# Split heads' q and k loaded one head beneath the other on 128 partitions, in a planned attention and two-layer MoE kernel

## The chip, the cores and the metric

The kernel runs on one core of a Trainium2 chip. The metric is the device time of one execution in microseconds; 1057.7 us is the median of three runs of the kernel before.

## What is computed

Causal attention with a decay from cumulative logs, then two gated feed-forward layers. Cut to what matters:

```python
B, H, S, D = 4, 8, 576, 64            # q, k, v: (B, H, S, D); f: (B, H, S)
scores = matmul(q, k.T) / sqrt(D)
cum = cumsum(log(clip(f, 1e-4, 1)), -1)
scores = where(causal, -1e9, scores + cum[..., :, None] - cum[..., None, :])
attn = softmax(scores)                 # the sum has 1e-9 added
x = concat_heads(attn @ v)             # (2304, 512)
x = (x @ w_a) * (x @ w_b) @ w_out      # d_ff 1536
xn = x / rms(x) * rms_g
out = silu(xn @ w_gate) * (xn @ w_val) @ w_out2
```

## The kernel before

The 2304 tokens are worked in three chunks of 576, 704 and 1024 columns, and each feed-forward layer runs per chunk as a phase: six phases on TensorE, which multiplies in a fast float format with 32-bit operands split into a high part and a remainder. The attention of batch 0 comes first; the attention of batches 1, 2 and 3 is woven between the matmuls of the phases (the table `ATT`), so that the softmax on VectorE and ScalarE runs beside feed-forward matmuls.

The order of all instructions on all engines is made at build time by the class `Plan`. Every piece of work is handed to `op` with its engine (or several to choose from), an estimated cost in ns, what it reads and writes, and a priority (a time: smaller goes first). `Plan.order` places the pieces one after the other: on each engine the piece that can start first, by estimated ends, latencies between engines, buffers that come free, and a lock between VectorE pieces marked `port=True` and GpSimd. A load is estimated in `run`: it ends at the later of its issue plus 1150 ns and the end of the load before it, plus its `nbytes` over `RATE` = 300 bytes per ns. Every 30,000 ns nine ways of weighing priorities are tried, and the one after which TensorE has done most is kept. All loads and stores are issued by SyncE, in the order of the plan, and a load that waits holds up those behind it.

Attention works by pairs of heads. `plan_attention` calls `heads` for each of the four pairs of a batch, and then `unit`, `packed` and `values`. `heads` makes the tiles of a pair: `b` (one buffer), `qk` (one buffer), `vr` (two). Batch 0 (`sf` true) multiplies 32-bit floats directly, and its q and k go straight into `b`. For the others ("split heads") q and k go into `qk`, and `head` builds from them, for each of the two heads g: `qa` (128 partitions: the high part of q in one half, the remainder of q in the other), `ka` (the high part of k in both halves), and rows 0 to 63 of `b` (high q, and the remainder of k; rows 64 to 67 come from a small load of decay rows). A score is then two matmuls: `qa` by `ka` over 128 rows, that is (high q + remainder of q) by high k, and `b` by `b` over 68 rows, that is high q by the remainder of k, and the decay.

The steps, as the prediction names them: the *loads* (L1889 to L1893, issued at L1873); the *copies*, which make high parts, by ScalarE (L1931) or GpSimd (L1933), whichever the plan expects to end first: first and second copy of q (L1942, L1943), first and second copy of k (L1948, L1949); and the *remainders* on VectorE (L1936): of q (L1944), which reads the first copy of q, and of k (L1950), which reads the second copy of k. Before, `qk` has q of both heads side by side on partitions 0 to 63 and k of both on 64 to 127, so that each load writes 64 partitions with two rows of up to 576 columns each.

Of the kernel before, what the change touches and what calls it, by code (L numbers as in the profile page):

```python
# [30 lines left out]
PE, ACT, DVE, POOL, SP = "PE", "ACT", "DVE", "POOL", "SP"  # L31
# [66 lines left out]
def act(n, psum=False):  # L98
    return (51 if psum else 93) + n / 1.2


def dve(n):
    return 69 + n / 0.96
# [10 lines left out]
def pool1(n):  # L114
    return 135 + n / 0.96
# [61 lines left out]
class Plan:  # L177
# [19 lines left out]
    def op(self, eng, cost, fn, reads=(), writes=(), prio=0.0, after=(), nbytes=0, start=0, port=False, kind=0):  # L197
        n = Node()
        n.port, n.kind = port, kind
        n.eng, n.cost, n.fn, n.prio, n.bytes, n.ready = eng, cost, fn, prio, nbytes, start  # L200
        deps, n.allocs, n.bufs, n.first = set(after), [], set(), set()
        for t in (*reads, *writes):
            b = t[0] if isinstance(t, tuple) and isinstance(t[0], Buf) else t
            if isinstance(b, Buf):
                if b.alloc is None:
                    b.alloc = n
                    n.allocs.append(b)
                    self.rings.setdefault(b.tag, []).append(b)
                elif b.alloc is not n:
                    n.first.add(b.alloc)  # L210
                if b not in n.bufs:
                    n.bufs.add(b)
                    b.users.append(n)
        for t in reads:
            assert t in self.writer, t
            deps.add(self.writer[t])
            self.readers.setdefault(t, []).append(n)
        for t in writes:
            if t in self.writer:
                deps.add(self.writer[t])  # L220
            deps.update(self.readers.get(t, ()))
            self.writer[t] = n
            self.readers[t] = []
        deps.discard(n)
        n.first -= deps
        deps |= n.first
        n.deps, n.outs, n.waiting = deps, [], len(deps)
        for d in deps:
            d.outs.append(n)
        n.given, n.att = (eng, cost, fn, start), False  # L230
        self.nodes.append(n)
        return n
# [153 lines left out]
class Kernel:  # L386
# [1479 lines left out]
    def heads(self, c, h, q0, k1, t, sf):  # L1866

        nc, op = self.nc, self.op
        g0 = c * H + h

        def load(cost, out, src, reads=(), writes=(), dt=0):
            op(
                SP, 600 if cost > 40000 else 320, lambda *_: nc.sync.dma_start(out(), src), reads=reads, writes=writes, prio=t - dt,  # L1873
                nbytes=cost, start=QUIET,
            )

        def of(x, rows, *at):
            return lambda: x.tile[(rows, slice(None), *at)]

        def heads_of(x, *at):  # L1880
            return x[(slice(g0, g0 + 2), *at)].rearrange("h d c -> d h c")

        both = range(2)
        top, dt = (66, F32) if sf else (68, F32R)
        b = self.tile([top, 2, 2, S], "b0", 2, dt, pool=self.early) if c == 0 else self.tile([top, 2, 2, S], "b", 1, dt, pool=self.att)
        qk = None if sf else self.tile([128, 2, S], "qk", 1, pool=self.att)
        vr = self.tile([128, 2, 5, D], "vr", 2, pool=self.att)
        for i, (x, lo) in enumerate(((self.qT, q0), (self.kT, 0))):
            out = of(b, slice(0, 64), i, slice(lo, k1)) if sf else of(qk, slice(64 * i, 64 * i + 64), slice(lo, k1))  # L1889
            load(  # L1890
                768 * (k1 - lo), out, heads_of(x, slice(None), slice(lo, k1)),
                writes=[(b, g, i, 0) if sf else (qk, g, i) for g in both], dt=15000,
            )  # L1893
        if sf:
            for i in both:
                load(
                    9216, lambda i=i: b.tile[64:66, :, i, :], heads_of(self.aux32, slice(i, i + 2), slice(None)),
                    [("aux32", 0), ("aux32", 1)], [(b, g, i, 1) for g in both], 12000,
                )
        else:  # L1900
            load(
                36864, lambda: b.tile[64:68].bitcast(F32).rearrange("p h t c -> p (h t) c"),
                self.aux[g0 : g0 + 2].rearrange("h t r c -> r (h t) c"), [("aux", i) for i in (0, 2, 4)],
                [(b, g, i, 1) for g in both for i in both], 12000,
            )
        nv = min(k1 // 128, 4)
        load(
            65536 * nv, lambda: vr.tile[:, :, 0:nv, :], self.vA[g0 : g0 + 2, :, 0:nv].rearrange("h p b d -> p h b d"),
            writes=[(vr, 0)], dt=11000,
        )  # L1910
        v = [(vr, 0)]
        if k1 > 512:
            load(
                32768, lambda: vr.tile[0:64, :, 4, :], self.vB[g0 : g0 + 2].rearrange("h p d -> p h d"), writes=[(vr, 1)],
                dt=10000,
            )
            v.append((vr, 1))
        return [self.head(g, q0, k1, t + 400 * g, sf, b, qk, vr, v) for g in both]

    def head(self, g, q0, k1, t, sf, b, qk, vr, v):  # L1920

        nc, op = self.nc, self.op
        pair = Slot(lambda: b.tile[:, g, 0]), Slot(lambda: b.tile[:, g, 1])
        own = [(b, g, i, j) for i in range(2) for j in range(2)]
        values = Slot(lambda: vr.tile[:, g]), v
        if sf:
            return [pair], own, values

        def copy(by, out, x):
            if by == ACT:  # L1930
                nc.scalar.activation(out, x, AF.Copy)  # L1931
            else:
                nc.gpsimd.tensor_scalar(out=out, in0=x, scalar1=1.0, scalar2=0.0, op0=ALU.mult, op1=ALU.add)  # L1933

        def rest(out, x, high):
            nc.vector.tensor_tensor(out=out, in0=x, in1=high.bitcast(F32), op=ALU.subtract)  # L1936

        qr, kr = (lambda: qk.tile[0:64, g]), (lambda: qk.tile[64:128, g])
        q, k = (qk, g, 0), (qk, g, 1)
        qa, ka = (self.tile([128, S], x + "a", 2, F32R, pool=self.att) for x in "qk")  # L1940
        n = k1 - q0
        op((ACT, POOL), (act(n), pool1(n)), lambda by, x: copy(by, x[0:64, q0:k1], qr()[:, q0:k1]), reads=[q], writes=[(qa, 0)], prio=t - 9000)  # L1942
        op((ACT, POOL), (act(n), pool1(n)), lambda by, *_: copy(by, b.tile[0:64, g, 0, q0:k1], qr()[:, q0:k1]), reads=[q], writes=[(b, g, 0, 0)], prio=t - 8000)  # L1943
        op(  # L1944
            DVE, dve(n), lambda: rest(qa.tile[64:128, q0:k1], qr()[:, q0:k1], qa.tile[0:64, q0:k1]),
            reads=[q, (qa, 0)], writes=[(qa, 1)], prio=t - 7000, port=True,
        )
        op((ACT, POOL), (act(k1), pool1(k1)), lambda by, x: copy(by, x[0:64, :k1], kr()[:, :k1]), reads=[k], writes=[(ka, 0)], prio=t - 7000)  # L1948
        op((ACT, POOL), (act(k1), pool1(k1)), lambda by, *_: copy(by, ka.tile[64:128, :k1], kr()[:, :k1]), reads=[k], writes=[(ka, 1)], prio=t - 6000)  # L1949
        op(  # L1950
            DVE, dve(k1), lambda: rest(b.tile[0:64, g, 1, :k1], kr()[:, :k1], ka.tile[64:128, :k1]),
            reads=[k, (ka, 1)], writes=[(b, g, 1, 0)], prio=t - 5000, port=True,
        )
        return [(qa, ka), pair], [*own, *((x, i) for x in (qa, ka) for i in range(2))], values

    def unit(self, c, u, heads, t, sf):

        a, e = u
        n, sm, ps = e - a, self.tile([128, 2], "sm", 4, pool=self.att), []
        for g, (pairs, qk, _) in enumerate(heads):  # L1960
            s = self.bank("s", S_BANKS)

            def scores(x, pairs=pairs):
                for j, (q, k) in enumerate(pairs):
                    self.nc.tensor.matmul(  # L1965
                        x[:n, :e], q.tile[:, a:e], k.tile[:, :e], start=j == 0, stop=j == len(pairs) - 1
                    )

            self.op(PE, 4 * e / 2.4 + 3 if sf else 2 * mm(e), scores, reads=qk, writes=[s], prio=t + 400 * g, kind=int(sf))
            p = self.tile([128, S], "P", P_BUFS, pool=self.att)  # L1970
            self.exps(n, e, [self.mask[:, 384 - a : 384 - a + e]], [s], p, sm, g, t + 600 + 400 * g)
            ps.append(p)
        self.norms(n, e, ps, sm, 1, t + 1000)
        return ps
# [192 lines left out]
```

## Time and profile before

| | |
|---|---|
| three runs | 1057.08, 1057.7, 1063.99 us |
| profiled execution, its time | 1057.13 us |
| its span, first to last instruction | 1055.4 us |
| TensorE matmul, busy | 1036.5 us (98%) |
| VectorE, busy | 830.3 us (79%) |
| ScalarE, busy | 605.6 us (57%) |
| GpSimd, busy | 193.2 us (18%) |
| mean granted clock of TensorE | 0.998 |

Busy times are sums over instructions of one engine. The ends of matmuls are modelled, so busy does not mean that TensorE runs at its peak. "PEld" is TensorE's weight load, which overlaps its matmuls. A wait is put down to the work that ended last before the waiting instruction began. The share of the DMA engines is a mean over sixteen; in short stretches it can read a little over 1.

### The profile page before, as it was taken

The page shows a single profiled execution, that of the slowest core. Times are in us where ns is not written, and L with a number is a line of the kernel's source. Part 1 is how long each engine was busy: PE and PEld are TensorE (multiplying, and loading weights), DVE is VectorE, ACT ScalarE, POOL GpSimd, SP SyncE. Part 2 cuts the span into 40 slices and gives each one's busy share as a digit, 9 for nine tenths or more (in the row PEclk, how much of TensorE's full clock was granted, in tenths as well). Part 3 has the DMA queues.
Part 4 walks back from the last instruction along what each step waited for, and adds up shares of the span by engine and source line. Part 5 has one row for each costly group of instructions (what it writes and reads, how often), then busy time and mean ns, then how long its engine had stood idle before and what let it go on. Part 6 is the DMA issues. An engine that isn't in the chain of part 4 may idle for free.

```text
span 1055.4 us, 19131 instructions
## 1 busy us (share of the span) xinstructions
PE 1036.5 (98%) x6716; PEld 931.0 (88%) x6716; DVE 830.3 (79%) x1877; ACT 605.6 (57%) x1324; POOL 193.2 (18%) x203
## 2 busy tenths in 40 slices
PE   9899999999999999999999999999999999999998
PEld 7688998899999998999999999988888887888886
DVE  7877989787597878977899587865568479979974
ACT  8889888755463779955775463532333264444330
POOL 3333333312101243333440010000000001100000
PEclk9999999999999999999999999999999999999999
DMA  7879787879486685787898684786453634546332
GB/s 180 270 246 300 245 284 244 256 238 347 158 295 233 223 281 191 234 281 260 289 319 307 227 282 173 273 278 194 138 180 120 206 115 152 178 130 191 119 118 80
DMA packets 90607, 233.05 MB, mean 221 GB/s; under 512 B 12960, under 2 KB 23408, under 8 KB 90512
## 3 DMA queue, kind: packets, MB, share of 16 engines
q1 hardware_dynamic: 90512, 231.84, 66.6%
q8 instruction: 53, 0.87, 0.3%
q14 instruction: 42, 0.34, 0.1%
HBM read 157.05 MB, written 74.74 MB: 220 GB/s over the span
## 4 chain that ended last, share of the span: by engine, by line
PE 62%; DVE 13%; ACT 9%; DMA 8%; issue 6%; POOL 2%; SPq 0%; DVEq 0%; POOLq 0%; ACTq 0%
PE m L940 15%; PE m L942 14%; PE m L941 14%; PE s L941 2%; PE s L942 2%; PE s L940 2%; ACT P L1562 2%; PE tp L941 2%; PE tp L942 2%; PE tp L940 2%; DMA raw<-wv 2%; DVE w L789 2%; DMA w<-wd 1%; PE tp L2029 1%; PE tp L1603 1%
## 5 line engine op out<-in xcount | busy, mean ns | idle before, releaser
L940 PE MATMUL m<-E,w 128*128 128x512 f32 (+3 forms) x672 | 233.3, 347 | 1.3 <-ACT a L1329 0.7
L942 PE MATMUL m<-E,w 128*128 128x512 f32 (+3 forms) x672 | 228.0, 339 | 0.5 <-POOL w L797 0.5
L941 PE MATMUL m<-E,w 128*128 128x512 f32 (+3 forms) x624 | 213.2, 342 | 0.0
L1329 ACT ACTIVATE a<-m 128x352 f32<-128x352 f32 (+1 forms) x144 | 74.7, 527 | 139.9 <-PE m L942 139.4
L941 PE MATMUL m<-Eb,w 128*128 128x352 f32 (+3 forms) x432 | 140.9, 326 | 0.0
L940 PEld LDWEIGHTS m<-E,w 128*128 128x128 f32 x672 | 127.3, 189 | 15.0 <-issue 1.4
L942 PEld LDWEIGHTS m<-E,w 128*128 128x128 f32 x672 | 126.9, 189 | 11.4 <-POOL w L797 0.9
L797 POOL TENSOR_TENSOR w<-w,w 128x512 fp32r<-128x512 f32 x72 | 97.1, 1354 | 201.7 <-ACT w L1654 161.3
L1338 DVE TENSOR_TENSOR a<-m,a 128x352 f32<-128x352 f32 (+1 forms) x144 | 86.3, 602 | 57.5 <-PE m L942 56.1
L940 PE MATMUL m<-Eb,w 128*128 128x352 f32 (+3 forms) x384 | 127.8, 333 | 1.2 <-ACT a L1329 0.6
L941 PEld LDWEIGHTS m<-E,w 128*128 128x128 f32 x624 | 118.2, 189 | 10.8
L942 PE MATMUL m<-Eb,w 128*128 128x352 f32 (+3 forms) x384 | 126.7, 330 | 0.0
L940 PE MATMUL m<-G,w 128*128 128x352 f32 (+2 forms) x352 | 111.3, 316 | 0.7 <-DVE a L1338 0.4
L941 PE MATMUL m<-G,w 128*128 128x352 f32 (+2 forms) x352 | 108.2, 308 | 0.0
L942 PE MATMUL m<-G,w 128*128 128x352 f32 (+2 forms) x352 | 108.2, 308 | 0.0
L1562 ACT ACTIVATE P<-P,mn 128x512 f32<-128x512 f32 (+4 forms) x128 | 76.3, 597 | 19.2 <-DVE mn L1555 19.0
L941 PEld LDWEIGHTS m<-Eb,w 128*128 128x128 f32 x432 | 81.3, 188 | 4.3
L940 PEld LDWEIGHTS m<-Eb,w 128*128 128x128 f32 x384 | 72.2, 188 | 6.9 <-ACT a L1329 0.8
L942 PEld LDWEIGHTS m<-Eb,w 128*128 128x128 f32 x384 | 72.2, 188 | 4.3
L1465 ACT ACTIVATE G<-a 128x352 fp32r<-128x352 f32 (+3 forms) x100 | 47.1, 473 | 46.1 <-DVE a L1451 17.8
L940 PEld LDWEIGHTS m<-G,w 128*128 128x128 f32 x352 | 66.2, 188 | 2.9 <-issue 1.7
L1555 DVE CUSTOM_DVE_ANT_0 P<-s,mask 128x512 f32<-128x512 f32 (+4 forms) x128 | 61.3, 494 | 9.1 <-PE s L1965 4.2
(264 smaller groups left out, 2262.4 us busy)
## 6 DMA issues: line engine op xcount, KB each, us to landing
w<-wd SPq DMA_DIRECT2D x72, 512.0 KB
wd<-w SPq DMA_DIRECT2D x48, 512.0 KB
ws<-w SPq DMA_DIRECT2D x48, 512.0 KB
w<-ws SPq DMA_DIRECT2D x48, 512.0 KB
w<-wf SPq DMA_DIRECT2D x60, 256.0 KB
wf<-w SPq DMA_DIRECT2D x48, 256.0 KB
raw<-wo SPq DMA_DIRECT2D x24, 512.0 KB
w<-wd SPq DMA_DIRECT2D x44, 256.0 KB
```

Of the source, the lines that this page charges most:

```text
L789: nc.vector.scalar_tensor_tensor(out=x, in0=words(I32, 0), scalar=29, in1=x, op0=ALU.logical_shift_right, op1=ALU.bitwise_or)
L797: nc.gpsimd.tensor_tensor(out=w.tile[:, :, 1, :], in0=i32.tile.bitcast(F32), in1=w.tile[:, :, 0, :].bitcast(F32), op=ALU.subtract)
L940: mm_(o, wh, xh, start=start, stop=False)
L941: mm_(o, wh, xl, start=False, stop=False)
L942: mm_(o, wl, xh, start=False, stop=stop)
L1329: nc.scalar.activation(z[:, :h], bank_.tile[:, :h], AF.Copy)
L1338: nc.vector.tensor_tensor(out=z, in0=bank_.tile[:, :h], in1=z, op=ALU.add)
L1465: nc.scalar.activation(out(0), x(), AF.Copy)
L1555: nc.vector.tensor_tensor_reduce(out=p.tile[:n, i * w : i * w + w], in0=s[i].tile[:n, :w], in1=masks[i][:n], scale=-0.125, scalar=mn.tile[ ...
L1562: nc.scalar.activation(o, o, AF.Exp, bias=mn.tile[:n, len(s) - 1 : len(s)], scale=-1.0, accum_out=sm.tile[:n, g : g + 1])
L1603: nc.tensor.transpose(ps.tile[:w, c : c + n], p.tile[:n, i * 128 : i * 128 + w], self.ident[:n, :n])
L2029: nc.tensor.matmul(x[64 * g : 64 * g + 64, o : o + n], tiles[g][2][0].tile[:k, i, :], y.tile[:k, to : to + n], start=i == 0, stop=i == blo ...
```

## The change

For split heads, q of the pair's two heads is now loaded one head beneath the other: head g lies on partitions 64g to 64g + 63, q in the first half of the tile's columns and k in the second, and each load writes 128 partitions with one row each. The estimate for the plan goes from 768 to 512 bytes per column; the estimated issue (600 ns over 40,000 bytes) stays, as all these loads are above it. In `head`, the high part of a head stands in the half where its raw data lie (`here`) and what is moved across stands in the other (`there`): for the first head that leaves q as it was, for the second head the halves of `qa` change places. The first copy of k goes to `here`, the second to `there`, and the remainder of k reads the first copy instead of the second. Rows 0 to 63 of `b` stay what they were.

```diff
         for i, (x, lo) in enumerate(((self.qT, q0), (self.kT, 0))):
-            out = of(b, slice(0, 64), i, slice(lo, k1)) if sf else of(qk, slice(64 * i, 64 * i + 64), slice(lo, k1))
+            if sf:
+                out, src = of(b, slice(0, 64), i, slice(lo, k1)), heads_of(x, slice(None), slice(lo, k1))
+            else:
+                out = lambda i=i, lo=lo: qk.tile[:, i, lo:k1]
+                src = x[g0 : g0 + 2, :, lo:k1].rearrange("h d c -> (h d) c")
             load(
-                768 * (k1 - lo), out, heads_of(x, slice(None), slice(lo, k1)),
-                writes=[(b, g, i, 0) if sf else (qk, g, i) for g in both], dt=15000,
+                (768 if sf else 512) * (k1 - lo), out, src, writes=[(b, g, i, 0) for g in both] if sf else [(qk, i)], dt=15000,
             )
...
-        qr, kr = (lambda: qk.tile[0:64, g]), (lambda: qk.tile[64:128, g])
-        q, k = (qk, g, 0), (qk, g, 1)
+        here, there = (slice(64 * x, 64 * x + 64) for x in (g, 1 - g))
+        qr, kr = (lambda i=i: qk.tile[here, i] for i in range(2))
+        q, k = (qk, 0), (qk, 1)
...
-            DVE, dve(n), lambda: rest(qa.tile[64:128, q0:k1], qr()[:, q0:k1], qa.tile[0:64, q0:k1]),
+            DVE, dve(n), lambda: rest(qa.tile[there, q0:k1], qr()[:, q0:k1], qa.tile[here, q0:k1]),
             reads=[q, (qa, 0)], writes=[(qa, 1)], prio=t - 7000, port=True,
         )
-        op((ACT, POOL), (act(k1), pool1(k1)), lambda by, x: copy(by, x[0:64, :k1], kr()[:, :k1]), reads=[k], writes=[(ka, 0)], prio=t - 7000)
-        op((ACT, POOL), (act(k1), pool1(k1)), lambda by, *_: copy(by, ka.tile[64:128, :k1], kr()[:, :k1]), reads=[k], writes=[(ka, 1)], prio=t - 6000)
+        op(*by_k, lambda by, x: copy(by, x[here, :k1], kr()[:, :k1]), reads=[k], writes=[(ka, 0)], prio=t - 7000)
+        op(*by_k, lambda by, *_: copy(by, ka.tile[there, :k1], kr()[:, :k1]), reads=[k], writes=[(ka, 1)], prio=t - 6000)
         op(
-            DVE, dve(k1), lambda: rest(b.tile[0:64, g, 1, :k1], kr()[:, :k1], ka.tile[64:128, :k1]),
-            reads=[k, (ka, 1)], writes=[(b, g, 1, 0)], prio=t - 5000, port=True,
+            DVE, dve(k1), lambda: rest(b.tile[0:64, g, 1, :k1], kr()[:, :k1], ka.tile[here, :k1]),
+            reads=[k, (ka, 0)], writes=[(b, g, 1, 0)], prio=t - 5000, port=True,
         )
```

## Rows read from the trace of the kernel before

**Rows 1.** Page, part 1: busy us, share of the span, instructions by engine.

```profile
PE 1036.5 (98%) x6716; PEld 931.0 (88%) x6716; DVE 830.3 (79%) x1877; ACT 605.6 (57%) x1324; POOL 193.2 (18%) x203
```

**Rows 2.** Stretches: length; PE, PEld, DVE, ACT, POOL busy; clock; DMA share, GB/s.

```profile
24.00:79.00 55.00, 52.10 (x432) 40.37 (x431) 45.69 (x128) 44.99 (x106) 19.50 (x19) 0.97 0.83 255
79.00:225.00 146.00, 141.27 (x1188) 132.88 (x1187) 122.41 (x336) 119.41 (x305) 46.32 (x51) 1.00 0.81 261
225.00:350.00 125.00, 124.36 (x840) 121.57 (x839) 94.93 (x236) 66.15 (x149) 17.26 (x22) 1.00 0.72 256
350.00:450.00 100.00, 98.13 (x814) 93.34 (x813) 87.80 (x228) 83.20 (x198) 36.58 (x38) 1.00 0.74 234
450.00:575.00 125.00, 123.88 (x965) 120.79 (x965) 105.85 (x259) 81.10 (x181) 42.83 (x40) 1.00 0.86 294
```

**Rows 3.** Waits of matmuls (PE), weight loads (PEld): us, times, longest.

```profile
PE tp L1603 <- ACT P L1586: 2.1, 3, 1.1
PE s L1965 <- DVE mn L1555: 2.0, 5, 0.7
...
PE m L940 <- DMA w<-wd: 0.6, 2, 0.4
...
PE s L1965 <- DVE b L1936: 0.3, 1, 0.3
...
PEld s L1965 <- DVE b L1936: 0.5, 1, 0.5
```

**Rows 4.** Instructions on tile qk: ns min/median/max, first and last start us, shapes.

```profile
L1936 DVE TENSOR_TENSOR qa<-qk,qa x32: 279/744/1836, 38.0 to 555.7; 64x576 fp32r<-64x576 f32 x16, 64x128 fp32r<-64x128 f32 x8, 64x448 fp32r<-64x448 f32 x8
L1936 DVE TENSOR_TENSOR b<-qk,ka x32: 284/753/1816, 43.4 to 563.7; 64x576 fp32r<-64x576 f32 x24, 64x128 fp32r<-64x128 f32 x8
...
L1873 SPq DMA_DIRECT2D qk<-kT x16: 595/602/610, 24.7 to 516.8; - x16
```

**Rows 5.** DMA issues of tile qk by size.

```profile
qk<-kT SPq DMA_DIRECT2D x12, 288.0 KB
...
qk<-qT SPq DMA_DIRECT2D x8, 288.0 KB
...
qk<-qT SPq DMA_DIRECT2D x4, 224.0 KB
...
qk<-qT SPq DMA_DIRECT2D x4, 64.0 KB
```

**Rows 6.** Stretches as in rows 2, beside and behind a pair's loads.

```profile
362.75:364.25 1.50, 1.50 (x13) 1.43 (x12) 1.44 (x4) 0.39 (x2) 0.00 (x0) 1.00 1.03 415
365.75:367.75 2.00, 1.88 (x12) 1.88 (x13) 2.00 (x8) 0.85 (x2) 0.00 (x0) 1.00 1.01 235
```

**Rows 7.** Waits for the loads of q and k: us, times, longest.

```profile
POOL qa L1933 <- DMA qk<-qT: 2.9, 1, 2.9
...
ACT ka L1931 <- DMA qk<-kT: 0.4, 1, 0.4
```

**Rows 8.** Issues at L1873: the load of v, columns as in rows 4.

```profile
L1873 SPq DMA_DIRECT2D vr<-vA x20: 378/386/1270, 14.2 to 526.2; - x20
```

**Rows 9.** Waits of SyncE's queue: us, times, longest.

```profile
SPq L1873 <- DVE b L1936: 30.6, 10, 8.2
```

**Rows 10.** Wide remainders and copies of k by shape: count, busy us, mean ns, idle before.

```profile
L1936 DVE TENSOR_TENSOR b<-qk,ka 64x576 fp32r<-64x576 f32 x24 | 19.1, 816 | 0.5
L1936 DVE TENSOR_TENSOR qa<-qk,qa 64x576 fp32r<-64x576 f32 x16 | 14.5, 930 | 0.3
...
L1933 POOL TENSOR_SCALAR ka<-qk 64x576 fp32r<-64x576 f32 x23 | 16.5, 715 | 9.7 <-issue 6.1 <-DMA qk<-kT 1.0 <-DMA w<-wd 0.7
...
L1931 ACT ACTIVATE ka<-qk 64x576 fp32r<-64x576 f32 x25 | 16.5, 680 | 0.8 <-DMA qk<-kT 0.4
```

**Rows 11.** Timeline of VectorE and GpSimd near 143 us: start us, us, what.

```profile
143.32 2.68 DVE L1936 TENSOR_TENSOR qa<-qk,qa 64x576 fp32r<-64x576 f32 x2
...
143.72 1.67 POOL L797 TENSOR_TENSOR w<-w,w 128x512 fp32r<-128x512 f32 x1
```

More of the change, by code (lines that the diff above doesn't have):

```diff
@@ L1936, in rest @@
             nc.vector.tensor_tensor(out=out, in0=x, in1=high.bitcast(F32), op=ALU.subtract)
-        qr, kr = (lambda: qk.tile[0:64, g]), (lambda: qk.tile[64:128, g])
-        q, k = (qk, g, 0), (qk, g, 1)
+        here, there = (slice(64 * x, 64 * x + 64) for x in (g, 1 - g))
+        qr, kr = (lambda i=i: qk.tile[here, i] for i in range(2))
+        q, k = (qk, 0), (qk, 1)
         qa, ka = (self.tile([128, S], x + "a", 2, F32R, pool=self.att) for x in "qk")
         n = k1 - q0
-        op((ACT, POOL), (act(n), pool1(n)), lambda by, x: copy(by, x[0:64, q0:k1], qr()[:, q0:k1]), reads=[q], writes=[(qa, 0)], prio=t - 9000)
-        op((ACT, POOL), (act(n), pool1(n)), lambda by, *_: copy(by, b.tile[0:64, g, 0, q0:k1], qr()[:, q0:k1]), reads=[q], writes=[(b, g, 0, 0)], prio=t - 8000)
+        by_q, by_k = ((ACT, POOL), (act(n), pool1(n))), ((ACT, POOL), (act(k1), pool1(k1)))
+        op(*by_q, lambda by, x: copy(by, x[here, q0:k1], qr()[:, q0:k1]), reads=[q], writes=[(qa, 0)], prio=t - 9000)
+        op(*by_q, lambda by, *_: copy(by, b.tile[0:64, g, 0, q0:k1], qr()[:, q0:k1]), reads=[q], writes=[(b, g, 0, 0)], prio=t - 8000)
         op(
-            DVE, dve(n), lambda: rest(qa.tile[64:128, q0:k1], qr()[:, q0:k1], qa.tile[0:64, q0:k1]),
+            DVE, dve(n), lambda: rest(qa.tile[there, q0:k1], qr()[:, q0:k1], qa.tile[here, q0:k1]),
             reads=[q, (qa, 0)], writes=[(qa, 1)], prio=t - 7000, port=True,
         )
-        op((ACT, POOL), (act(k1), pool1(k1)), lambda by, x: copy(by, x[0:64, :k1], kr()[:, :k1]), reads=[k], writes=[(ka, 0)], prio=t - 7000)
-        op((ACT, POOL), (act(k1), pool1(k1)), lambda by, *_: copy(by, ka.tile[64:128, :k1], kr()[:, :k1]), reads=[k], writes=[(ka, 1)], prio=t - 6000)
-        op(
-            DVE, dve(k1), lambda: rest(b.tile[0:64, g, 1, :k1], kr()[:, :k1], ka.tile[64:128, :k1]),
-            reads=[k, (ka, 1)], writes=[(b, g, 1, 0)], prio=t - 5000, port=True,
+        op(*by_k, lambda by, x: copy(by, x[here, :k1], kr()[:, :k1]), reads=[k], writes=[(ka, 0)], prio=t - 7000)
+        op(*by_k, lambda by, *_: copy(by, ka.tile[there, :k1], kr()[:, :k1]), reads=[k], writes=[(ka, 1)], prio=t - 6000)
+        op(
+            DVE, dve(k1), lambda: rest(b.tile[0:64, g, 1, :k1], kr()[:, :k1], ka.tile[here, :k1]),
+            reads=[k, (ka, 0)], writes=[(b, g, 1, 0)], prio=t - 5000, port=True,
         )
```

## The prediction

> **What bounds the kernel now.** I read the busy times first. TensorE is busy 1036.5 of 1055.4 us [rows 1]. The count of matmuls and their shapes depend on no line of this diff, so the change can only touch the 18.9 us in which TensorE stands idle, or add to them. I then cut the span into stretches around the split heads (the first k is loaded at 24.7 us, the last at 516.8, and the last remainder starts at 563.7 us [rows 4]). In [rows 2] the first column after the length is TensorE's busy time, so its idle time is 55.00 - 52.10 = 2.90, 146.00 - 141.27 = 4.73, 125.00 - 124.36 = 0.64, 100.00 - 98.13 = 1.87 and 125.00 - 123.88 = 1.12 us: 11.3 us over the 551 us from 24 to 575. The rest of the idle time lies before 24 us or behind 575 us, where no split head is prepared. Third, the waits of TensorE by releaser: the longest sums are 2.0 and 2.1 us, for the softmax of the attention; the only wait of a matmul for what the diff edits is 0.3 us, once, for the remainder of k, and a weight load, which overlaps matmuls, waits 0.5 us for the same [rows 3]. No row has TensorE waiting for the load of q or k. So the kernel is bound by TensorE's own work, and the edited work has TensorE waiting for fractions of a microsecond.
>
> **The change part by part.**
>
> *The loads.* 32 DMAs: 12 of k and 8 of q with 288 KB, 4 of q with 224 KB, 4 of q and as many of k with 64 KB, that is 20 x 294,912 + 4 x 229,376 + 8 x 65,536 = 7.34 MB [rows 5]. None is added and no byte more is moved; each now spans 128 partitions instead of 64. Does that make them shorter? The stretch 365.75 to 367.75 us follows the issue of a q and a k load, and the DMA engines are full (share 1.01) but move 235 GB/s; 362.75 to 364.25 us, where weights on 128 partitions are under way, is as full and moves 415 GB/s [rows 6]. I take these two as the rates before and after: 294,912 B take 1.25 us, then 0.71 us, 0.54 us less for each wide load, and 7.34 MB take 31.2, then 17.7 us, 13.5 us less of DMA time in all. From below the saving is nothing (if the low rate is due to what else was in flight); I take the measured ratio, since nothing but the span differs in kind. What hides it: the code gives each load a lead of 15,000 ns on its head. Only GpSimd and ScalarE have rows of waiting for them, five rows from 2.9 down to 0.4 us [rows 7], and TensorE has none. What TensorE can get back through the shorter queue is bounded by its waits for any DMA, 0.6 us for a weight tile [rows 3]. I book 0.3 us.
>
> *Their issue on SyncE.* A load of k takes 602 ns to issue [rows 4], one of v, already on 128 partitions, 386 ns [rows 8]. If the new form takes the latter, 32 x 0.216 = 6.9 us of SyncE's queue are saved; if not, nothing. SyncE's queue waits 30.6 us for the remainder of k to release the q and k tile [rows 9]; behind those loads in order stand v, the auxiliary rows and the next weights. All this is slack that TensorE doesn't see (its DMA waits are the same 0.6 us), so it is booked at nothing.
>
> *The copies and remainders.* Per head four copies and two remainders, before as after, with the same shapes; only the partition halves change. Copies from 64-127 to 0-63 exist before; the move from 0-63 to 64-127 by ScalarE or GpSimd is new, and I bound it by the same rows: 680 ns on ScalarE, 715 on GpSimd [rows 10], no reason for another length. Booked at nothing.
>
> *The remainder of k waits for the first copy of k instead of the second.* At best it starts one copy (0.68 to 0.72 us) sooner. TensorE's wait behind it was 0.3 us, so at most 0.3 us comes back. It also loses a protection. The remainder of q already waits for its first copy alone, and takes 930 ns in the wide form, where that of k takes 816 [rows 10]; the longest are 1836 and 1816 ns against medians of 744 and 753 [rows 4]. In the timeline the cause is visible: two remainders of q take 2.68 us from 143.32 to 146.00, beside a GpSimd instruction that runs from 143.72 to 145.39 [rows 11]. Taken at the price of q, the 24 wide remainders of k cost 24 x 0.114 = 2.7 us of VectorE; nothing from below, 24 x (1.816 - 0.816) = 24.0 us from above. VectorE is busy 122.41 of 146 and 87.80 of 100 us in the two stretches where most of them run [rows 2], so most of 2.7 us stays hidden; I book +0.2 us.
>
> The Trainium skill says, in "SBUF — State Buffer", section "Who interferes with whom", that "A DVE instruction with two SBUF inputs contends with a GpSimd instruction that reads SBUF". By that rule the earlier start of k's remainder is dangerous just when the second copy falls to GpSimd; the trace agrees (2.68 us for the two in [rows 11]), and by the rule alone the sum would lean to the slower rival below.
>
> *The order of everything.* The kernel orders all its instructions at build time from estimated costs. The estimate of a load falls from 768 to 512 bytes per column, at 300 bytes per ns from 1.47 to 0.98 us for 576 columns. So everything behind the first loads at 24 us may be placed anew, on all engines. This has no row; it is bounded by how well the same order does in its own stretches. With TensorE's idle share of the best stretch, 0.64/125 = 0.5%, the 551 us would have 2.8 us of idle time instead of 11.3: 8.5 us faster, 1048.6. With that of 79 to 225 us, 4.73/146 = 3.2%, they would have 17.9: 6.6 us slower, 1063.7. I take no change, being nearest to the whole of the rows, and keep both ends.
>
> Sum: 1057.1 (the profiled execution; its span is 1055.4 and 1.7 us lie around it) - 0.3 - 0.3 + 0.2 - 0 = 1056.7. The median of the runs shown is 1057.7, so 0.6 us more would be as good a number. I say **1056.7 us**, no change that can be told.
>
> **The rivals.**
>
> *The shorter loads pay.* The order with earlier data closes the gaps around the attention in 79 to 225 us and the total falls to 1048.6 us as worked out above. For it: 4.73 of the 11.3 us lie where most of the loads lie, and the DMA engines are 81% busy there [rows 2]. Against: TensorE's waits name the softmax, which no line of the diff shortens. Even with all 11.3 us gone it would be 1045.8, just over 1% below.
>
> *The remainder of k collides with GpSimd.* Place: VectorE between 79 and 225 and between 350 and 450 us. Price: up to 24.0 us of VectorE; if half of it reaches TensorE, 1057.1 + 12.0 = 1069.1 us. It decides when each of the 32 remainders makes TensorE wait 10.6/32 = 0.33 us, where now its matmuls wait 0.3 us for all together. Against: the build-time order keeps GpSimd and this VectorE instruction apart in its own estimate, and the remainder of q, which runs without the protection, makes no matmul wait in the view of [rows 3].
>
> *The new order is worse.* At the idle share of 79 to 225 us throughout: 1063.7 us. For it: nothing in the diff steers the order; against: it optimises the same score as before, with slightly smaller costs.
>
> *The load isn't shorter after all.* Then 31.2 us of DMA time stay, the order is changed all the same, and the time is 1057 us. It can't be told from my forecast by time, only by the rates.
>
> **How the numbers follow.** Forecast, the last rival with it: 0.64. Shorter loads pay: 0.14, of which 0.04 end over 1% (10.6 us) below. Collision: 0.09, of which 0.06 end over 1% above. Worse order: 0.13, of which 0.02 do. About 1% is what a measurement of this kernel tells from no change. That makes faster 0.04, same 0.88, slower 0.08. The range leaves out the collision and the outermost of the other two: 1048.6 to 1063.7. The forecast's own range is 1053 to 1061, a third of the way and somewhat more to those ends.
>
> **What would show it.** The issue of a q or k load near 390 ns and over 350 GB/s while two of them are in flight show the load step right. Copies near 680 and 715 ns and as many as before show theirs. The remainder of k between 0.82 and 0.93 us in the wide form, and TensorE's waits for it under 1 us, show that step; over 1.2 us on average would be the rival. TensorE busy near 1036 us and 9 to 13 us idle between 24 and 575 us show that the new order is as good as the old. I am wrong if that idle time is below 3 or above 22 us, or if TensorE's busy time itself moves by several us.

## The result: half a per cent slower

The kernel after takes 1063.84 us (median of 20 runs, 1061.38 to 1067.78), the kernel before, run beside it, 1058.83 (20 runs, 1056.01 to 1063.99): a ratio of 1.0051 with a 95% interval of [1.004, 1.0062], 5.0 us more. That is inside the 1% that the prediction called "same", but not the "no change" that it forecast, and the median lies 0.1 us beyond the end of its range. Below, ratios are always to the kernel before in the same set of runs; its median in the sets is 1058.8 to 1061.0 us, so medians of different sets compare less well than ratios.

The profiled execution after took 1066.82 us, 3.0 above its own median, that of before 1057.13, 1.7 below its own. So the two traces show a difference of 9.7 us, twice what is to be explained; single waits are read from them, sums only with care.

The page after, part 1 as in [rows 1] (busy us by engine) and the line of part 3 for the queue of all loads and stores (packets, MB, share of 16 engines over the span):

```profile
PE 1042.0 (98%) x6716; PEld 934.8 (88%) x6716; DVE 833.7 (78%) x1879; ACT 603.8 (57%) x1310; POOL 204.0 (19%) x215
...
q1 hardware_dynamic: 90512, 231.84, 65.3%
```

The same 6716 matmuls are busy 5.5 us longer, and TensorE is idle 1065.0 - 1042.0 = 23.0 us instead of 18.9. The stretches, columns as in [rows 2], show both:

```profile
24.00:79.00 55.00, 51.05 (x402) 38.31 (x400) 42.70 (x125) 43.18 (x100) 19.57 (x17) 0.91 0.78 237
79.00:225.00 146.00, 139.90 (x1176) 131.69 (x1175) 121.91 (x334) 116.75 (x293) 52.15 (x61) 0.99 0.77 258
225.00:350.00 125.00, 124.43 (x844) 122.07 (x844) 93.79 (x235) 63.32 (x142) 18.06 (x23) 1.00 0.71 256
350.00:450.00 100.00, 97.99 (x787) 93.45 (x786) 86.45 (x234) 79.34 (x188) 33.61 (x34) 1.00 0.70 239
450.00:575.00 125.00, 122.93 (x959) 118.61 (x958) 105.69 (x248) 84.86 (x188) 45.67 (x43) 1.00 0.85 280
```

The granted clock in the first of them is 0.91 where it was 0.97. Matmuls last longer there, so busy time grows: 30 fewer are done in the same 55 us (402 against 432). Over the span the mean clock is 0.993 against 0.998, that is 7.5 against 2.1 us of missing full-rate time, and the difference of 5.4 is close to the added busy time. Idle time between 24 and 575 us is 3.95 + 6.10 + 0.57 + 2.01 + 2.07 = 14.7 us against 11.3.

What the edit itself changed is as hoped. The issues of q and k on SyncE, columns as in [rows 4]:

```profile
L1873 SPq DMA_DIRECT2D qk<-qT x16: 328/333/597, 24.1 to 520.7; - x16
L1873 SPq DMA_DIRECT2D qk<-kT x16: 328/424/594, 24.7 to 521.1; - x16
```

One pair's loads are issued at 426.21 and 426.59 us; while they are under way, with nothing else in flight, the full DMA engines move 392 GB/s (columns as in [rows 6], where 235 was read with a load of v in flight as well). The same microsecond of the same pair in the old layout, from the kernel of experiment 1 that has the order of after, stands second, with 277:

```profile
428.00:429.00 1.00, 0.79 (x8) 0.55 (x6) 1.00 (x4) 0.93 (x4) 0.00 (x0) 1.00 1.01 392
```

```profile
428.00:429.00 1.00, 0.29 (x4) 0.06 (x2) 1.00 (x5) 0.93 (x2) 0.00 (x0) 1.00 1.06 277
```

And the remainders and copies by shape, as in [rows 10] (the helper lines 1931, 1933 and 1936 of before are 1934, 1936 and 1939 now):

```profile
L1939 DVE TENSOR_TENSOR b<-qk,ka 64x576 fp32r<-64x576 f32 x24 | 20.3, 847 | 0.5
L1936 POOL TENSOR_SCALAR ka<-qk 64x576 fp32r<-64x576 f32 x23 | 18.8, 818 | 12.2 <-PE s L1970 10.9
L1934 ACT ACTIVATE ka<-qk 64x576 fp32r<-64x576 f32 x25 | 17.0, 681 | 0.4
L1939 DVE TENSOR_TENSOR qa<-qk,qa 64x576 fp32r<-64x576 f32 x16 | 14.2, 888 | 3.9 <-POOL qa L1936 3.5
```

The last row holds a new wait: VectorE stood idle 3.5 us, once, for the first copy of q on GpSimd. The timeline (start us, us, what, idle before and its releaser) shows where. VectorE near 29 us:

```profile
29.45 0.75 DVE L1939 TENSOR_TENSOR qa<-qk,qa 64x576 fp32r<-64x576 f32 x1 [3.48 <-POOL qa L1936]
30.23 0.17 DVE L1579 RECIPROCAL sm<-sm 128x1 f32<-128x1 f32 x1
```

ScalarE and TensorE there:

```profile
28.70 0.68 ACT L1934 ACTIVATE qa<-qk 64x576 fp32r<-64x576 f32 x1 [2.29 <-DMA qk<-qT]
...
31.32 0.77 PE L1603 MATMUL tp<-ident,P 128*128 128x128 f32 x5 [1.89 <-ACT P L1586]
```

The first q of batch 1 was issued at 24.1 us and its data came at 28.7. The new order put its remainder onto VectorE right behind the load; before, the first remainder of q stood at 38.0 us [rows 4]. So VectorE and ScalarE waited for the load, the reciprocal of batch 0's softmax waited behind the remainder, the transpose behind that softmax, and TensorE had nothing for 1.89 us. The windows of 5 us around it (columns as in [rows 2], the granted clock last but two):

```profile
25.00:30.00 5.00, 4.43 (x29) 3.33 (x27) 1.27 (x4) 2.66 (x7) 1.53 (x3) 1.00 0.99 268
30.00:35.00 5.00, 3.09 (x21) 1.75 (x23) 4.22 (x14) 4.95 (x11) 1.40 (x2) 0.85 0.72 271
35.00:40.00 5.00, 4.71 (x28) 3.02 (x25) 3.56 (x12) 3.86 (x10) 2.21 (x2) 0.50 0.88 228
40.00:45.00 5.00, 5.00 (x25) 4.30 (x24) 3.89 (x15) 3.50 (x10) 1.44 (x2) 0.63 0.62 226
```

TensorE is busy 4.43 and 3.09 of 5 us, and then runs at the lower of its two levels (1.2 instead of 2.4 GHz) for about 10 us. Before, the clock is full from 25 to 45 us and low only for some 3 us behind 50:

```profile
35.00:40.00 5.00, 5.00 (x28) 3.52 (x27) 4.94 (x13) 4.72 (x12) 2.63 (x3) 1.00 0.64 203
...
50.00:55.00 5.00, 3.91 (x19) 3.52 (x20) 3.99 (x13) 3.72 (x9) 0.08 (x1) 0.70 0.50 149
```

Behind 450 us there is a second new wait (waits of matmuls between 450 and 660 us: us, times, longest; after, then before):

```profile
PE m L940 <- ACT a L1329: 2.0, 2, 1.7
```

```profile
PE m L940 <- ACT a L1329: 0.6, 1, 0.6
```

The trace after has waits as long between 79 and 225 us (2.0 and 1.5 us, transposes behind the softmax). They aren't in the trace of the kernel of experiment 1 with the same order, which has the two named here (3.6 us on VectorE, 1.5 us behind 450 us); so they belong to one execution.

So three suspects: the layout, the order near 29 us with the clock behind it, and the order later on.

### The profile page after: what moved, and what is told of

Same layout as the page of the kernel before. It is cut to its first block, busy times and chain, and to the rows that moved or that the text cites. A ratio compares the mean times of both kernels' runs of the same rounds, so it can differ in the third digit from the quotient of the medians.

```text
span 1065.0 us, 19113 instructions
## 1 busy us (share of the span) xinstructions
PE 1042.0 (98%) x6716; PEld 934.8 (88%) x6716; DVE 833.7 (78%) x1879; ACT 603.8 (57%) x1310; POOL 204.0 (19%) x215
## 3 DMA queue, kind: packets, MB, share of 16 engines
q1 hardware_dynamic: 90512, 231.84, 65.3%
## 5 line engine op out<-in xcount | busy, mean ns | idle before, releaser
L1329 ACT ACTIVATE a<-m 128x352 f32<-128x352 f32 (+1 forms) x144 | 74.5, 526 | 140.6 <-PE m L942 140.1
```

The source lines that it names most:

```text
L1329: nc.scalar.activation(z[:, :h], bank_.tile[:, :h], AF.Copy)
```

## Experiments

Each kernel was timed against the kernel before, in 6 to 12 runs. None leaves out work; one adds some.

**1. Layout or order.** Two kernels cross them. The first has the new loads and halves in the order of before: the estimate back at 768, and the remainder of k behind the second copy. So that it still reads what it waits for, the two copies of k change places:

```diff
-                (768 if sf else 512) * (k1 - lo), out, src, ...
+                768 * (k1 - lo), out, src, ...
...
-        op(*by_k, ... copy(by, x[here, :k1], ...), writes=[(ka, 0)], ...)
-        op(*by_k, ... copy(by, ka.tile[there, :k1], ...), writes=[(ka, 1)], ...)
+        op(*by_k, ... copy(by, x[there, :k1], ...), writes=[(ka, 0)], ...)
+        op(*by_k, ... copy(by, ka.tile[here, :k1], ...), writes=[(ka, 1)], ...)
-            reads=[k, (ka, 0)], writes=[(b, g, 1, 0)], ...
+            reads=[k, (ka, 1)], writes=[(b, g, 1, 0)], ...
```

> The new layout of q and k, with the estimate put back to 768 bytes per column and the remainder of k put back behind the second copy of k (the first copy now goes to the half it does not read): the order of instructions on TensorE, VectorE, ScalarE and GpSimd is that of the kernel before, word for word. Theory 1 (the order costs the time): as the kernel before, 1058 to 1059 us, clock below full for about 3.4 us only, q and k loads issued in 0.33 to 0.43 us. Theory 2 (the layout itself costs it: moves across halves, the new form of load): near the changed kernel, 1063 to 1064 us. Theory 3 (both): between, near 1061 us.

Measured: 1058.96 against 1058.82 us, ratio 1.0001 [0.9986, 1.0016]. The second has the old loads in the order of after, by the same edit the other way round in the kernel before (512, remainder of k behind the first copy):

> The mirror of the first: the old layout on 64 partitions per load, with the estimate of 512 bytes per column and the remainder of k behind the first copy: the order on all four engines is that of the changed kernel. Theory 1 (order): 1063 to 1065 us, with VectorE waiting some 3.5 us near 26 us and the clock below full for about 10 us from 33 us on. Theory 2 (layout): 1058 to 1059 us. Should the longer loads add to the wait, somewhat above the changed kernel, up to 1066 us.

Measured: 1064.76 against 1058.82 us, 1.0058 [1.0035, 1.0082], with VectorE waiting 3.6 us for the same copy. So the layout costs or gains nothing that can be told (0.16% at most), and the loss sits in the order, which the loads' real length has no part in.

**2. Which input of the order.** Two inputs of the plan changed: the estimate (768 to 512) and the dependency of k's remainder (second to first copy). Each was put back alone; the first by the upper half of the diff above, the second by its lower half.

> The changed kernel with the estimate alone put back to 768 bytes per column; the remainder of k still follows the first copy of k. The order is that of the kernel before up to about 100 us and differs behind it. Theory 1a (the estimate of the load, which brings the first split head forward at 25 us, costs the time): 1057 to 1060 us, no long wait of VectorE near 26 us. Theory 1b (the earlier remainder of k costs it, by collisions with GpSimd): 1062 to 1065 us and remainders of k above 900 ns on average in the wide form.

> The changed kernel with the estimate of 512 kept, and the remainder of k put back behind the second copy. The order is that of the changed kernel up to about 100 us. Theory 1a (the estimate costs the time): 1062 to 1065 us, with the wait of VectorE near 26 us and the clock below full from 33 us on for about 10 us. Theory 1b (the remainder of k): 1057 to 1060 us.

Measured: with 768, 1055.11 us, 0.9966 [0.9952, 0.998]; with the second copy, 1064.3 us, 1.0054 [1.0034, 1.0073]. The estimate is what costs: with 768 the new layout and the new dependency are 3.6 us faster than the kernel before, below both theories of that kernel and the lowest ratio of all versions. The dependency costs nothing at either value: 1055.11 with the first copy against 1058.96 us with the second at 768, 1063.84 against 1064.3 at 512. Why it goes with a gain at 768 alone isn't read from a wait; that order differs too.

**3. The wait near 29 us and the clock.** One theory: the early remainder of q, and the clock that falls behind its gap, are most of the loss. Three kernels test it. The first holds the six pieces that prepare each head of the first split pair until 29,000 ns of the plan:

```diff
-        return [self.head(g, q0, k1, t + 400 * g, sf, b, qk, vr, v) for g in both]
+        return [self.head(g, q0, k1, t + 400 * g, sf, b, qk, vr, v, 29000 if g0 == H else 0) for g in both]
...
-            reads=[q, (qa, 0)], writes=[(qa, 1)], prio=t - 7000, port=True,
+            reads=[q, (qa, 0)], writes=[(qa, 1)], prio=t - 7000, start=start, port=True,
```

> The changed kernel, 512 bytes per column everywhere, but the copies and remainders of the first split pair may not be placed before 29.0 us in the plan, which is where its q landed in the profile of the changed kernel (28.7 us). The rest of the order is made anew. Theory 1 (the early place of that one pair, ahead of data that have not landed, costs the time): no wait of VectorE over 1 us between 24 and 32 us, clock full from 33 to 44 us, 1055 to 1060 us. Theory 2 (512 bytes mislead the order all along): 1062 to 1065 us.

Measured: 1064.74 us, 1.0055 [1.0035, 1.0076]. VectorE's wait for the copy of q is gone, but the time is not back: another order came with it, in which VectorE waits 3.6 us for a transpose, and the mean clock is 0.994. The second puts the estimate of 512 into the kernel before, for that first pair alone:

```diff
-                768 * (k1 - lo), out, heads_of(x, slice(None), slice(lo, k1)),
+                (512 if g0 == H else 768) * (k1 - lo), out, heads_of(x, slice(None), slice(lo, k1)),
```

> The kernel before with the suspected cause put in: the loads of the first split pair alone are estimated at 512 bytes per column, all others at 768, old layout and old dependency. The first remainder of q then stands at the early place on VectorE, as in the changed kernel. Theory 1: VectorE waits about 3 us near 26 us, TensorE behind it, the clock falls, 1062 to 1065 us. Theory 2 (the rest of the order): 1057 to 1060 us.

Measured: 1060.95 us, 1.002 [1.0006, 1.0035]. The early remainder is there (VectorE waits 3.5 us, once) and the mean clock is 0.993, as after; the loss is 2.0 us of 5.0. The third leaves the order of after as it is and repeats score matmuls of two units of the first attention where the gap lies, so that TensorE is busy through it. The added matmuls are superfluous:

```diff
-                for j, (q, k) in enumerate(pairs):
+                self.scored = getattr(self, "scored", 0) + 1
+                for j, (q, k) in list(enumerate(pairs)) * {3: 5, 4: 2}.get(self.scored, 1):
```

> The changed kernel, order untouched, with TensorE's gaps behind the late softmax filled: the scores matmul that ends at 29.4 us is issued five times instead of once (four more, about 1.7 us, for a gap of 1.9 us), the next one twice. The work added is superfluous and starts each result anew; nobody waits for it sooner. Theory A (most of the loss is the clock that falls after the gap: about 10 us at half rate, so 5 us): clock full from 33 to 44 us, 1058 to 1061 us. Theory B (the gap and the late instructions themselves cost the time, the clock only follows): 1063 to 1066 us whatever the clock shows.

It does what it should for the clock; the windows of this kernel, as above:

```profile
30.00:35.00 5.00, 5.00 (x18) 2.28 (x18) 3.15 (x9) 4.08 (x10) 0.25 (x1) 1.00 0.45 175
35.00:40.00 5.00, 4.30 (x41) 2.92 (x42) 4.17 (x15) 3.66 (x10) 1.98 (x2) 1.00 0.62 123
40.00:45.00 5.00, 4.85 (x34) 4.05 (x34) 4.80 (x15) 4.06 (x11) 1.34 (x2) 1.00 0.88 337
```

With TensorE busy 5.00 of the 5 us, the clock stays at 1.00 right where it fell to 0.50. Yet the time is 1063.86 us, 1.0042 [1.0028, 1.0055]: the clock does what theory A asked, the time falls into the range of theory B. The means are 1063.3 for this kernel and 1064.3 us for after, 4.2 and 4.7 above the kernel before in the same sets, so 0.5 to 1.0 us are gained. How much is that? The mean clock of its nine runs leaves 1.2 us of missing full-rate time, that of after's twenty 6.0, so 4.8 us came back on TensorE. But the filling has a price, which the timeline of TensorE shows. After, and with the gap filled:

```profile
27.77 1.67 PE L1970 MATMUL s<-b 66*128 66x384 f32 x4
31.32 0.77 PE L1603 MATMUL tp<-ident,P 128*128 128x128 f32 x5 [1.89 <-ACT P L1586]
31.92 1.02 PE L1970 MATMUL s<-b 66*128 66x512 f32 x2
```

```profile
27.63 5.10 PE L1971 MATMUL s<-b 66*128 66x384 f32 x12
32.57 0.71 PE L1603 MATMUL tp<-ident,P 128*128 128x128 f32 x5
33.12 1.88 PE L1971 MATMUL s<-b 66*128 66x512 f32 x4
```

The first four matmuls became twelve, eight more where the expectation counted four, and the two behind the transposes four: 5.10 - 1.67 + 1.88 - 1.02 = 4.3 us added, of which 1.9 lie in the gap and 2.4 don't. If those 2.4 are paid in full, the clock's return is worth 2.9 to 3.4 us, an estimate, since both means are uncertain by about a microsecond. That is less than the 4.8 us of the records and something like two thirds of the loss. The clock is a real part of it; whether it is most of it the three kernels don't tell, since the one with only the early wait loses 2.0 us.

**4. Which part of the run.** The estimate can be set by batch (`c` is the batch): 512 for batch 3 alone, or for batches 1 and 2 alone. The two orders are those of the 768 kernel and of after, in this sequence, up to about 350 us.

```diff
-                (768 if sf else 512) * (k1 - lo), out, src, ...
+                (768 if sf or c < 3 else 512) * (k1 - lo), out, src, ...     (512 late)
+                (768 if sf or c == 3 else 512) * (k1 - lo), out, src, ...    (512 early)
```

> The changed kernel with 768 bytes per column for the split pairs of batches 1 and 2 and 512 for those of batch 3. The order is that of the run with 768 throughout (1055.1 us) up to about 350 us and new behind it. Theory 1 (some 2 us are lost with the first split pair at 25 us, the other 3 us behind 450 us by what 512 does there): 1057.5 to 1059 us. Theory 2 (all is lost before 100 us, gap and clock): 1054 to 1056 us. Theory 3 (each new order is a new draw, with no rule): anywhere from 1053 to 1060 us.

> The reverse: 512 for batches 1 and 2, 768 for batch 3. The order is that of the changed kernel up to about 350 us and new behind it, so the wait of VectorE near 26 us and the fall of the clock are in it. Theory 1: 1060 to 1061.5 us. Theory 2: 1063 to 1065 us. Theory 3: 1059 to 1065 us, with the idle time of TensorE between 450 and 660 us not smaller than in the changed kernel.

Measured: late 1061.2 us, 1.0027 [1.0013, 1.0041]; early 1058.25 us, 0.9996 [0.9983, 1.0009]. With the two that were there:

| | batch 3 at 768 | batch 3 at 512 |
|---|---|---|
| batches 1, 2 at 768 | 1055.11 | 1061.2 |
| batches 1, 2 at 512 | 1058.25 | 1063.84 |

The early part costs 3.1 or 2.6 us, the late part 6.1 or 5.6 (by the ratios 3.2 or 2.5 and 6.5 or 5.8, each uncertain by about 2 us): additive as far as can be told. These are parts of the 8.7 us above 768, not of the 5.0 above the kernel before. The early part is of the size that experiment 3 gave the clock, and the mean clock goes with it (0.995 over the twelve runs with 512 early, 0.999 late). The larger part is the late one, which no theory had: late came out above all three ranges, early below them. The theory that the wait near 29 us and the clock are most of the loss falls here: with 512 early, which has both (VectorE waits 2.7 us), the time is that of the kernel before, and without them, with 512 late alone, it is 6.1 us above 768. The wait of the matmuls for ScalarE's copy at L1329, seen after, is there with 512 late (the same view):

```profile
PE m L940 <- ACT a L1329: 1.6, 1, 1.6
PE m L940 <- DMA w<-wd: 1.1, 1, 1.1
```

With 768 throughout the longest wait of that stretch is 0.4 us:

```profile
PE tp L2034 <- ACT pt L2081: 0.4, 1, 0.4
```

and with 512 early likewise:

```profile
PE m L1533 <- DVE xn L1500: 0.4, 1, 0.4
```

Idle TensorE time from 350 to 660 us is 2.3 us with 768, 1.6 with 512 early, 6.4 with 512 late and 6.1 after. The stretch 450 to 575 us alone, 768 throughout first and 512 late second (columns as in [rows 2]):

```profile
450.00:575.00 125.00, 124.29 (x967) 121.37 (x966) 109.29 (x257) 84.33 (x186) 42.44 (x39) 1.00 0.82 287
```

```profile
450.00:575.00 125.00, 121.10 (x960) 116.57 (x957) 105.93 (x248) 82.12 (x182) 45.40 (x42) 1.00 0.87 292
```

The clock is 1.00 in both: this part is plain waiting. What waits, from the timeline after: VectorE does the last pair's remainders and weights' remainders in between, the gated product comes late from it, and ScalarE stands idle for it before the copy that TensorE wants. VectorE and then ScalarE:

```profile
574.94 1.32 DVE L1939 TENSOR_TENSOR qa<-qk,qa 64x576 fp32r<-64x576 f32 x1
576.29 1.11 DVE L858 TENSOR_TENSOR w<-w,w 128x512 fp32r<-128x512 f32 x1
577.33 1.05 DVE L1468 TENSOR_TENSOR G<-a,G 128x352 fp32r<-128x352 f32 x1
...
579.77 0.51 DVE L1417 TENSOR_TENSOR a<-m,a 128x352 f32<-128x352 f32 x1
580.21 0.74 DVE L1939 TENSOR_TENSOR b<-qk,ka 64x576 fp32r<-64x576 f32 x1
...
580.32 0.50 ACT L1465 ACTIVATE G<-a 128x352 fp32r<-128x352 f32 x1 [2.45 <-DVE a L1417]
580.72 0.45 ACT L1329 ACTIVATE a<-m 128x352 f32<-128x352 f32 x1
```

**5. Which pair of the late part.** Batch 3 was split: 512 for its last pair alone (`h < 6` added to the condition for 768), and for its first three alone (`h == 6`).

> 768 bytes per column for all split pairs but the last of batch 3, which has 512. The order is that of 768 throughout (1055.1 us) up to about 410 us. If the 6 us of the run with 512 for batch 3 come from the waits behind 540 us, around the last pair, because that pair is expected earlier: 1059 to 1062 us, with the 1.6 us wait of TensorE for the scaling on ScalarE (a at L1329) near 575 us. If they come from each new order being a draw: anywhere from 1053 to 1060 us, with that wait absent.

> The reverse: in batch 3 the first three pairs have 512, the last 768; batches 1 and 2 have 768. The order is that of the run with 512 for batch 3 (1061.2 us) up to about 480 us and new behind it. If the loss sits around the last pair: 1055 to 1057.5 us, TensorE idle less than 3 us between 450 and 660 us. If it sits before it: 1060 to 1062 us.

Measured: 1058.9 us, 0.9976 [0.996, 0.9993], and 1059.04 us, 0.9983 [0.9964, 1.0001]; the kernel before had 1061.02 in this set. At 1058.8 for the kernel before, these ratios are 1056.3 and 1057.0 us. Neither alone brings the loss, and neither has the wait (0.2 us at most for that releaser). The late loss belongs to an order that arises from both together, not to one pair. That the wait is the whole of it isn't shown: it is 1.7 us of some 4 more idle, and other waits differ too. Nor does idle time in one trace tell the loss: with 752 bytes throughout (experiment 6) TensorE is idle 5.6 us from 350 to 660 us, and that kernel isn't slower than the one before.

**6. How fine the estimate acts.** Three more values in place of 512, with the rest of after (640 here, then 752 and 784):

```diff
-                (768 if sf else 512) * (k1 - lo), out, src, ...
+                (768 if sf else 640) * (k1 - lo), out, src, ...
```

> The changed kernel with an estimate of 640 bytes per column, between the two. The order places the first remainder of q behind 30 us. Theory 1: as the time goes by whether that instruction stands ahead of its data, there is no long wait of VectorE near 26 us and the time is 1055 to 1060 us. Theory 2 (the smaller the estimate the worse the order throughout): 1060 to 1062 us.

> The changed kernel with 752 bytes per column: 2% less than the 768 that gave 1055.1 us, a difference of about 30 ns in the estimate of a wide load. The order is new from about 25 us on. Theory 3 (each new order is a draw): a time off 1055.1 by 2 us or more, either way. Theory 1 and 2 (the time goes by how early the loads are expected): within 1.5 us of 1055.1.

> The changed kernel with 784 bytes per column, 2% more than 768. As for 752: theory 3 has it off 1055.1 us by 2 us or more, either way; theories 1 and 2 within 1.5 us of it. If it is below 1055 us, it is the fastest so far.

| bytes per column | us | ratio to before |
|---|---|---|
| 512 (after) | 1063.84 | 1.0051 [1.004, 1.0062] |
| 640 | 1057.76 | 0.9988 [0.9972, 1.0004] |
| 752 | 1057.84 | 0.9989 [0.9971, 1.0007] |
| 768 | 1055.11 | 0.9966 [0.9952, 0.998] |
| 784 | 1057.61 | 0.9976 [0.996, 0.9991] |

A change of 2% in the estimate of one sort of load moves the median up by 2.5 to 2.7 us on either side; by the ratios it is 2.4 us against 752, with intervals that overlap a little, and 1.1 against 784, which is within the noise. From 640 to 752 nothing moves; 640 came out as theory 1 had it, 752 as theory 3, and 784 as either, by its median or by its ratio. 512 is clearly the worst of the five. Whether the other four scatter, or get a little better with a larger estimate, they don't decide. That an order's worth isn't a sum of its parts rests on other pairs: the halves of experiment 5, which lose nothing alone, and the dependency, worth 3.9 us with 768 and nothing with 512.

## Why the prediction was wrong, by its steps

*The loads* were right in kind: 392 GB/s with a pair's loads under way, where over 350 was named. The size was too large: the step took 235 to 415 GB/s from stretches with other loads in flight, and the same pair alone goes from 277 to 392. By these rates 7.34 MB take 26.5, then 18.7 us: 7.8 us less (an estimate), where the step had 13.5. The Trainium skill names a reason in "SBUF — State Buffer", section "Door 1: The DMA port swizzle": partitions 0 to 63 reach only half of the memory's DMA ports. The trace agrees in direction; no run here separates that from the two rows per partition becoming one. Over all loads and stores, 66.6% of 1055.4 us is 702.9 us of DMA time before, 65.3% of 1059.8 us is 692.0 in the new layout with the old order: 10.9 us less, other transfers' times included. That nearly none of it would reach TensorE was right as well: 1.0001 in experiment 1.

*Their issue* fell from 602 to 333 ns (q) and 424 ns (k), on either side of the 386 expected, and brought nothing, as booked.

*Copies and remainders.* On ScalarE a copy of k takes 681 ns, 680 before, on GpSimd 818 instead of 715: 23 x 0.103 = 2.4 us of GpSimd, and no wait of a matmul names a copy. The longer copies go with the order and not with the halves: the new layout in the old order has 709 ns, the old layout in the new order 822. The Trainium skill's rule ("SBUF — State Buffer", section "Who interferes with whom"), which the prediction weighed, agrees with two more places (start us, us, what), where the one that starts second takes longer. At 574.94 us the remainder of q starts 0.03 us behind an instruction of GpSimd and takes 1.32 us; at 29.45 it starts 0.08 us ahead of two copies on GpSimd and takes 0.75, and the copies take 1.95, against 0.67 for one just before:

```profile
28.75 0.67 POOL L1936 TENSOR_SCALAR qa<-qk 64x576 fp32r<-64x576 f32 x1 [3.35 <-DMA qk<-qT]
29.53 1.95 POOL L1936 TENSOR_SCALAR ka<-qk 64x576 fp32r<-64x576 f32 x2
...
574.91 0.74 POOL L847 TENSOR_TENSOR w<-w 128x256 f32<-128x256 f32 x1 [6.96 <-DVE a L1406]
```

*The remainder of k* in the wide form takes 847 ns, between the 816 and 930 named, and matmuls waited 0.9 us for it, under the 1 us that was to hold:

```profile
PE s L1994 <- DVE b L1939: 0.9, 1, 0.9
```

The collision rival (1.2 us each) did not come.

*The order of everything* is the step that failed. It was booked at nothing, "I take no change, being nearest to the whole of the rows", the middle of two bounds, and the new order cost 5.0 us (1.0051; 1.0058 with the old layout). The time of the rival "the new order is worse", 1063.7 us with a chance of 0.13, is the one that came, and its mechanism isn't: TensorE is idle 14.7 us from 24 to 575 us, not 17.9, and 5.5 of the 9.7 us between the traces are TensorE's own busy time at a lower clock. That the bound has the right size is luck. With it the first step fails in part: "the change can only touch the 18.9 us in which TensorE stands idle" left out that a new order can change how long the same matmuls take, although [rows 2] had a clock of 0.97 in the first stretch; one of the prediction's own signs of being wrong, busy time that moves by several us, came. A part of the miss is no mechanism at all: the sum began at one execution of 1057.1 us, and the median of twenty is 1058.83, so 1.7 of the 7.1 us between 1056.7 and 1063.84 are its base. The re-made orders of the experiments have ratios from 0.9966 to 1.0058: the step should have said that an order re-made at build time is worth several microseconds either way, more than all other terms of the sum (0.3, 0.3, 0.2) together. "It optimises the same score as before" was an argument against a loss that carried no weight: the score is the plan's, and the plan's ends differ from the chip's. Near 29 us the reason can be read: by the plan's formula a load of 576 columns issued at 24.1 us, with nothing ahead of it, ends 1.15 + 0.98 us later, at 26.2, and on the chip the data came at 28.7, with the DMA engines busy 0.99 of the time from 25 to 30 us. With 768 bytes the formula gives 26.7, which is also too early; that the 0.5 us tip the order is shown by the kernel of experiment 3 with 512 for that pair alone, where the remainder starts at 29.3 us, while with 640 for all it starts at 33.3. The smaller estimate describes the transfer better, and the wait for it no better: it moved the plan's end further from the chip's.

What stays open: the price of the clock. The records have 4.8 us more of missing full-rate time with 512 than without the gap, the filled gap returns an estimated 2.9 to 3.4, and the early half of the change costs 2.6 to 3.1; and with an estimate of 640 the clock is missing 4.3 us and the time is 1057.76 all the same. That the other engines catch up while TensorE is slow, so that later waits shrink, would fit, and is only argued. Open too is which difference of the late orders, besides the wait of 1.7 us, carries the rest of the 6 us.

## What to carry to other kernels

In a kernel whose order is made from estimates, an edit of one estimate is an edit of everything behind it: cost it apart from the edit of the hardware work, with a spread taken from several values, and give that spread the chances. Before a layout is judged, cross it with the order (new work in the old order, old work in the new); here that took two kernels and settled it. And keep the estimate as something to be tried: the same layout was 0.5% slower with the estimate that describes it better and 0.34% faster with the old one.

## What the runs showed of the hardware

Spreading a load over 128 partitions instead of 64, with the same bytes, took the issue on SyncE from 602 to 333 and 424 ns and the rate of a pair's loads with full DMA engines from 277 to 392 GB/s, and left the kernel's time as it was (1.0001). Behind a gap of 1.9 us in which TensorE had nothing it ran for about 10 us at half the clock, and with matmuls put into the gap it didn't. And single executions mislead at this size: the profiled ones of after and of the kernel with the gap filled lie 4.5 us apart (1066.82 and 1062.36), their medians 0.02, and the runs of one kernel spread over 2 to 10 us.
